# Eight heads per K/V tile and model vectors as rows, in a one-core decode block with adaptive layer norm, cached attention and a gated FFN

## The chip, the core and the metric

The kernel runs on one core of a Trainium2 chip. The core has a matrix engine (PE; its weight loads are shown apart, as PEld), a vector engine (DVE), a scalar engine (ACT), GpSimd (POOL), a queue engine (SP) that issues most transfers, and 16 DMA engines that bring data from device memory (HBM) into the on-chip memory of 128 partitions. Matmul results go to a second memory, PSUM, of eight banks. The metric is the device time of one execution in microseconds; lower is better.

## The reference, cut to what matters

Two tokens (batch `B` = 2, one position each) of width `D` = 640 go through one block. A conditioning vector `c` gives six vectors of width 640 per token. Attention has 32 heads of width 192; each head has its own cache, of which the last `W` = 1024 positions are used. The FFN is 1536 wide.

```python
mod = (silu(c) @ w_mod).reshape(2, 6, 1, -1)
sa, ca, ga, sb, cb, gb = (mod[:, i] for i in range(6))
h = layernorm(x) * (1 + ca) + sa
q = (h @ wq).reshape(2, 1, 32, 192).transpose(0, 2, 1, 3)
k, v = k_cache[:, :, -1024:], v_cache[:, :, -1024:]
p = softmax(einsum('bhqd,bhkd->bhqk', q, k) * 192 ** -0.5)
x = x + ga * (einsum('bhqk,bhkd->bhqd', p, v).transpose(0, 2, 1, 3).reshape(2, 1, 6144) @ wo)
h = layernorm(x) * (1 + cb) + sb
x = x + gb * ((gelu(h @ w_gate) * (h @ w_up)) @ w_down)
```

The caches' part is 50.3 MB, `wq` and `wo` 7.9 MB each, `w_mod` 4.9 MB, the three FFN matrices 2.0 MB each: 76.9 MB in all, each byte read once.

## The kernel before

**Order of work.** The program is a list of operations, each with an engine, the buffers it reads and writes, and a name. Each engine runs its own operations in the order in which they were listed, and waits (L93) for those of other engines that it depends on. So the order of the listing is the order of every queue. SP issues the transfers (L231) and, in its own order, waits for the slot that a transfer will fill.

**Stages.** `w_mod` comes first, then `wq` in five pieces, then K and V, `wo` in six pieces, `w_gate`, `w_up`, and `w_down` in three pieces. Vectors of width 640 are kept as columns: 128 partitions, five values each per token. `mod_part` (L359), the `wo` product (L556) and the `down` product (L606) therefore load a 128x128 piece of the weights into PE and stream two columns (the tokens) through it. `ln_norm` makes the layer norm's sums with one matmul against ones (L311) and a chain of small DVE operations; `ln_mod` applies scale and shift and gives the columns that the next product streams. The q product (L382) is turned round: the two token columns are the loaded operand, `wq` streams, in four column tiles of PE side by side (partitions 0, 32, 64, 96 of the output). `q_unit` spreads q over the partitions, two of the eight units before the loop and the rest within it.

**Ring.** `wq`, K, V and `wo` pass through a ring of `NS` = 8 slots of 12 KB per partition. A slot is refilled by the item eight places later in `items`, once its reader is done (`declare_ring`).

**Attention loop.** One K or V tile holds `HQ` = 4 heads of one token; a partition holds 32 consecutive positions of one head, one run of 12,288 bytes. There are `NG` = 16 groups. For group g, DVE multiplies K by q (`d_mul`, L419) in three pieces of 16, 8 and 8 positions; PE sums each piece over the head width with 12 matmuls against the identity (`p_reduce`, L432); DVE finishes the sum (L439) and takes a maximum (L442); PE transposes it (L444), DVE takes the maximum per head (L449), PE spreads it (L458, L459), DVE subtracts it (L464), ACT takes the exponent and its sum (L467); PE adds the sums over partitions (L473) and multiplies with V (`p_pv`, L484, four column tiles); DVE inverts the sum (L493), ACT scales the result (L495), and PE places it (`p_sel`, L507). The loop at L514 is written out as a pipeline of three groups: while DVE multiplies group g's three pieces, the sum, maximum and subtraction of group g-1 stand between the pieces, and inversion and placing of group g-2 too.

**Tail.** The ACT copy of all heads' result (L546), `wo` (L556), the residual (L574, L577), the second layer norm, gate and up products (`ffn_gu`, L587, 60 load-and-matmul pairs each, weight columns 12 elements apart), GELU (L594), the gating product (L598), the down product (L606), the last residual (L612, L615), and one transfer of the result (L617).

Of the kernel before, what the change touches and what calls it, by code (L numbers as in the profile page):

```python
# [103 lines left out]
def bass_adaLN_cond__sliding_block_cached__geglu_ffn__decode_kernel(  # L104
# [22 lines left out]
    HQ = 4  # L127
# [5 lines left out]
    DD = Dh // NT  # L133
    FC = F // P
    assert B == 2 and D == KT * P and J * PH == W and NQD * HQ == H and NT * P == NQ
    assert DD * NT == Dh and DD * H == P and FC * P == F and J % 8 == 0
# [3 lines left out]
    GC = 512 // J  # L140
    NCH = Dh // GC
    assert GC * NCH == Dh
# [3 lines left out]
    NS = 8  # L146
    SLOT = J * Dh
    assert SLOT == NQ
    WOT = 8
    NWO = NT // WOT  # L150
    assert NWO * WOT == NT and WOT * D <= SLOT
    CHUNKS = [(0, J // 2), (J // 2, J // 4), (3 * J // 4, J // 4)]
    WD_SPLIT = [(0, 6), (6, 4), (10, 2)]
    assert FC == 12
    X0 = HQ * DD * (NQD - 1) + DD - 1
    ZW = X0 + DD * (HQ - 1) + P
    QW = 2 * Dh
    NQB = NQ // (HQ * QW)

    es = ExitStack()  # L160
    with es:
# [10 lines left out]
        prod = sb("prod", [P, 2, J, Dh], BF16)  # L172
        qbc = sb("qbc", [P, B, NQD, Dh], BF16)
        qrow = sb("qrow", [P, NQ // HQ], BF16)
# [4 lines left out]
        mask4 = sb("mask4", [P, HQ], F32)  # L179
        mneg = sb("mneg", [P, HQ], BF16)  # L180
        maskc = sb("maskc", [P, P], F32)
        selq = sb("selq", [P, B, P], BF16)
        ztmp = sb("ztmp", [P, 4, 2, HQ], BF16)
        zsel = sb("zsel", [P, 2, ZW], BF16)
        rows = sb("rows", [2 * B, D], BF16)
        scT = sb("scT", [P, KT, B], BF16)
        X2 = sb("X2", [P, 2, KT, B], F32)
        st4 = sb("st4", [P, 4], F32)
        mv = sb("mv", [P, 8], F32)
        rstd = sb("rstd", [P, 2], F32)  # L190
        modT = sb("modT", [P, 6, KT, B], F32)
        opc = sb("opc", [P, 2, KT, B], F32)
        lnt = sb("lnt", [P, 2, KT, B], F32)
# [13 lines left out]
        fin = sb("fin", [P, KT, B], F32)  # L207
        finb = sb("finb", [P, B, KT], BF16)
        ps = es.enter_context(nc.psum_tensor("ps", [P, 8, 512], F32))

        BK_S = (0, 1)
        BK_Q = (2, 3)
# [3 lines left out]
        BK_M = 7  # L216

# [3 lines left out]
        sem_x = S.sem("d_x")  # L221
# [6 lines left out]
        sem_out = S.sem("d_out")  # L228
# [4 lines left out]
        items = [("wq", k) for k in range(KT)] + [("k", 0)]  # L233
        for g in range(1, NG):
            items += [("k", g), ("v", g - 1)]
        items += [("v", NG - 1)] + [("wo", i) for i in range(NWO)]
# [6 lines left out]
        def ring_src(it):  # L243
            kind, i = it
            if kind == "wq":
                return A_wq.rearrange("(p k) n -> p k n", k=KT)[:, i, :], NQ
            if kind == "wo":
                return A_wo.rearrange("(p t) n -> p t n", t=NT)[:, i * WOT:(i + 1) * WOT, :].rearrange("p t n -> p (t n)"), WOT * D
            quad, b = group(i)
            src = A_k_cache if kind == "k" else A_v_cache  # L250
            return src[b, quad * HQ:(quad + 1) * HQ, K0:Sk, :].rearrange("h (p j) d -> p h (j d)", p=PH), SLOT

        def declare_ring(consumed=()):
            ring_state["done"].update(consumed)
            while ring_state["next"] < len(items):
# [8 lines left out]
        S.dma("act", k_dma(rows[0:B, :], c[:, :]), sem_c, writes=["rows"], name="ld_c")  # L264
        S.dma("act", k_dma(rows[B:2 * B, :], A_x.rearrange("b o d -> (b o) d")), sem_x, writes=["rows_x"], name="ld_x")
        wm_dma = S.dma("sp", k_dma(wm_v.rearrange("p k n -> p (k n)"), w_mod.rearrange("(p k) n -> p (k n)", k=KT)), sem_wm,
                       writes=["wm"], name="ld_wm")
        declare_ring()

# [6 lines left out]
             reads=["ident_f"], writes=["ident_b"], name="ident_b")  # L276
        for b in range(B):
            S.op("pool", lambda e, b=b: e.affine_select(out=selq[:, b, :].rearrange("p (x h) -> p x h", h=HQ),
                                                        in_=ones_b[:, 0:1].unsqueeze(2).broadcast_to([P, PH, HQ]),
                                                        pattern=[[0, PH], [-32, HQ]],  # L280
                                                        compare_op=ALU.is_equal, fill=0.0, base=-b, channel_multiplier=1),
                 reads=["ones_b"], writes=[("selq", b)], name="selq%d" % b)
        S.op("pool", lambda e: e.affine_select(out=ztmp[:, :, :, :].rearrange("p i q h -> p i (q h)"),
                                                in_=ones_b[:, 0:1].unsqueeze(2).broadcast_to([P, 4, 2 * HQ]),
                                                pattern=[[-32, 4], [-1, 2 * HQ]],
# [4 lines left out]
        S.op("dve", lambda e: e.memset(ps[:, 0:4, 0:QW], 0.0), writes=[bank(k) for k in range(4)], name="init_Q")  # L290
        S.op("dve", lambda e: e.memset(ps[:, BK_O, 0:ON], 0.0), writes=[bank(BK_O)], name="init_O")
        S.op("dve", lambda e: e.tensor_reduce(out=mask4[:, :], in_=ident_f[:, :].rearrange("p (x h) -> p h x", h=HQ), axis=AX.X, op=ALU.add),
             reads=["ident_f"], writes=["mask4"], name="mask4")

        cx_ps = ps[:, BK_M, 256:256 + 2 * KT].bitcast(BF16).rearrange("p (j r) -> p j r", j=KT)

        def cx_T(e):
            last = None
            for j in range(KT):
                last = e.transpose(cx_ps[:, j, :], rows[:, :].rearrange("r (p j) -> r p j", j=KT)[:, :, j], ident_b[0:2 * B, 0:2 * B])  # L300
            return last
        S.op("pe", cx_T, reads=["rows", "rows_x", "ident_b"], writes=[bank(BK_M)], name="cxT")
        S.op("act", lambda e: e.activation(out=scT[:, :, :], in_=cx_ps[:, :, 0:B], func=ACTF.Silu),
             reads=[bank(BK_M)], writes=["scT"], name="silu")
        S.op("dve", lambda e: e.tensor_copy(out=X2[:, 0, :, :], in_=cx_ps[:, :, B:2 * B]),
             reads=[bank(BK_M)], writes=[("X2", 0)], name="x_f32")

        def ln_norm(tag):
            S.op("dve", lambda e: e.tensor_tensor(out=X2[:, 1, :, :], in0=X2[:, 0, :, :], in1=X2[:, 0, :, :], op=ALU.mult),
                 reads=[("X2", 0)], writes=[("X2", 1)], name=tag + "_sq")  # L310
            S.op("pe", lambda e: e.matmul(ps[:, BK_M, 448:448 + 4 * KT], lhsT=ones_f[:, :],  # L311
                                          rhs=X2[:, :, :, :].rearrange("p q j b -> p (q j b)"), start=True, stop=True),
                 reads=[("X2", 0), ("X2", 1), "ones_f"], writes=[bank(BK_M)], name=tag + "_stat")
            S.op("dve", lambda e: e.tensor_reduce(out=st4[:, :].rearrange("p (q b) -> p q b", q=2),
                                                  in_=ps[:, BK_M, 448:448 + 4 * KT].rearrange("p (q j b) -> p q b j", q=2, j=KT),
                                                  axis=AX.X, op=ALU.add),
                 reads=[bank(BK_M)], writes=["st4"], name=tag + "_sum")
            S.op("dve", lambda e: e.tensor_scalar(out=mv[:, 0:4], in0=st4[:, :], scalar1=1.0 / D, scalar2=None, op0=ALU.mult),
                 reads=["st4"], writes=[("mv", 0)], name=tag + "_mean")
# [15 lines left out]
        def ln_mod(tag, opc_idx, s_idx, dst_bf):  # L335
# [13 lines left out]
             reads=["ztmp", "zsel"], writes=["zsel"], name="zsel")  # L349

        mod_pe = []

        def mod_part(part, i0, i1):
            def f(e):
                last = None
# [43 lines left out]
        def q_unit():  # L399
            if qstate["n"] >= len(qunits):  # L400
                return
# [268 lines left out]
```

## Time and profile before

| what | value |
|---|---|
| time, median of 3 runs | 195.16 us (195.07 to 195.35) |
| the profiled execution's own time | 194.89 us |
| its span, first to last instruction | 193.1 us |
| bytes read from HBM | 76.88 MB, 398 GB/s over the span |
| busy: PE, DVE, ACT | 124.5, 86.4, 28.3 us |
| mean clock granted to PE | 0.862 of full speed |
| second piece of `wq` done to third, third to fourth, fourth to fifth: starts of the q product | 26.98, 30.67, 34.36 us |
| DVE starts on K of group 0, of group 1 | 38.01, 41.69 us |
| DVE starts on K of group 15 | 146.48 us |
| last piece of `wo` is multiplied | 172.50 to 174.26 us |
| `w_gate` product, `w_up` product | 177.77 to 181.52, 181.80 to 185.56 us |
| result's transfer is issued | 188.90 us |

An instruction group is listed with its line, engine, operation, what it writes and reads, its shape and count, and then its busy time, the mean length of one, and the idle time before it with what ended that. In a chain of waits each step goes back to what released the step after it. The granted clock is written down by the profiler from 44.1 us on; what stands before that as full speed has no record behind it.

### The profile page before, as it was taken

What the parts mean: (1) busy time and instruction counts of PE and PEld (TensorE: products, weight loads), DVE (VectorE), ACT (ScalarE), POOL (GpSimd) and SP (SyncE); (2) the same over time, 40 slices, a digit from 0 to 9 for tenths busy, and PEclk for the clock granted to TensorE, in tenths of its full rate; (3) what the DMA queues carried; (4) which work ended last, traced back from release to release, by engine and by line L of the source; (5) the groups of instructions that cost most, each with busy time, mean ns of one, the idle gap of its engine ahead of it and who ended that gap; (6) DMA issues with size and microseconds to landing.
All of it is one profiled execution on the core that took longest, in us unless ns stands there. A gap on an engine that the chain in (4) does not pass through costs nothing.

```text
span 193.1 us, 3891 instructions
## 1 busy us (share of the span) xinstructions
PE 124.5 (64%) x1723; PEld 95.2 (49%) x1723; DVE 86.4 (45%) x164; ACT 28.3 (15%) x70; POOL 2.6 (1%) x12
## 2 busy tenths in 40 slices
PE   0108932479768777597597586596595858563990
PEld 0108600158446556475375355384374538463990
DVE  3221000396847747658649549559556600004000
ACT  2300000303211312201101101201111231003000
POOL 5000000000000000000000000000000000000000
PEclk9999999999996999969879999969969975555555
DMA  7999999999999999999999999999999999999910
GB/s 255 438 392 428 426 428 425 423 428 428 428 421 428 426 425 419 431 417 433 416 433 420 426 422 422 428 422 428 421 425 428 420 415 431 414 435 423 378 71 1
DMA packets 7353, 77.13 MB, mean 399 GB/s; under 512 B 1060, under 2 KB 1064, under 8 KB 1448
## 3 DMA queue, kind: packets, MB, share of 16 engines
q1 hardware_dynamic: 7328, 76.88, 94.7%
q8 instruction: 13, 0.21, 0.4%
q14 instruction: 4, 0.03, 0.0%
q10 hardware_dynamic: 8, 0.01, 0.0%
HBM read 76.88 MB, written 0.00 MB: 398 GB/s over the span
## 4 chain that ended last, share of the span: by engine, by line
DMA 81%; DVE 6%; PE 6%; issue 3%; SPq 1%; DVEq 0%
DMA ring<-in_A_k_cache_dram 53%; DMA r<-in_B_w_up_dram 15%; DMA ring<-in_A_wq_dram 13%; DVE prod L419 4%; PE ps L587 2%; PE ps L432 1%; PE ps L606 1%; SPq L231 1%; DVE S_sb L439 1%; PE ps L382 1%; DVE nmx L449 0%; DVE M L442 0%; DVE rden L493 0%; DVE aT L598 0%; DVE finb L615 0%
## 5 line engine op out<-in xcount | busy, mean ns | idle before, releaser
L432 PE MATMUL ps<-prod,ident_b 128*128 128x128 bf16 (+1 forms) x576 | 59.1, 261 | 28.1 <-DVE prod L419 28.0
L419 DVE TENSOR_TENSOR prod<-ring,qbc 128x1536 bf16<-128x1536 bf16 (+1 forms) x48 | 58.1, 1214 | 26.4 <-DMA ring<-in_A_k_cache_dram 26.4
L432 PEld LDWEIGHTS ps<-prod,ident_b 128*128 128x128 bf16 x576 | 45.3, 108 | 42.4 <-DVE prod L419 37.8
L495 ACT ACTIVATE On<-ps,rden 128x384 bf16<-128x384 f32 x16 | 9.3, 580 | 42.8 <-DVE rden L493 39.5
L556 PE MATMUL ps<-oT,ring 128*128 128x2 bf16 x240 | 10.4, 179 | 5.3 <-DMA ring<-in_A_wo_dram 4.9
L484 PE MATMUL ps<-ring,E_sb 128*8 128x384 bf16 x256 | 13.4, 330 | 0.0
L556 PEld LDWEIGHTS ps<-oT,ring 128*128 128x128 bf16 x240 | 10.0, 131 | 5.8 <-DMA ring<-in_A_wo_dram 5.2
L467 ACT ACTIVATE E_sb<-Sb_sb 128x128 bf16<-128x128 f32 x16 | 4.9, 309 | 47.1 <-DVE Sb_sb L464 47.1
L382 PE MATMUL ps<-ring,hT 128*2 128x384 bf16 x80 | 7.1, 517 | 7.2 <-DMA ring<-in_A_wq_dram 7.2
L439 DVE TENSOR_REDUCE S_sb<-ps 128x32 f32<-128x512 f32 x16 | 10.8, 673 | 1.3 <-PE ps L432 1.3
L359 PE MATMUL ps<-scT,r 128*128 128x2 bf16 x150 | 6.3, 179 | 6.4 <-DMA r<-in_w_mod_dram 6.2
L359 PEld LDWEIGHTS ps<-scT,r 128*128 128x128 bf16 x150 | 6.2, 131 | 6.6 <-issue 6.3
L587 PE MATMUL ps<-h2T,r 128*128 128x2 bf16 x120 | 7.5, 199 | 2.5 <-DVE h2T L338 2.2
L587 PEld LDWEIGHTS ps<-h2T,r 128*128 128x128 bf16 x120 | 7.3, 164 | 2.7 <-DVE h2T L338 2.3
L574 DVE TENSOR_TENSOR lnt<-ps,modT 128x10 f32<-128x10 f32 x1 | 0.2, 169 | 17.9 <-PE ps L556 17.9
L473 PE MATMUL ps<-denp,maskc 128*128 128x1 f32 x32 | 6.1, 260 | 3.0 <-ACT E_sb L467 2.6
L382 PEld LDWEIGHTS ps<-ring,hT 128*2 128x2 bf16 x80 | 2.1, 108 | 11.5 <-DMA ring<-in_A_wq_dram 9.5
L464 DVE TENSOR_TENSOR Sb_sb<-S_sb,ps 128x128 f32<-128x128 f32 x16 | 4.6, 288 | 6.4 <-PE ps L459 6.4
L473 PEld LDWEIGHTS ps<-denp,maskc 128*128 128x128 f32 x32 | 4.8, 188 | 5.3 <-ACT E_sb L467 5.2
L393 DVE CAST qrow<-ps 128x384 bf16<-128x384 f32 x2 | 1.0, 553 | 13.8 <-PE ps L382 13.8
L458 PE MATMUL ps<-nmx,ones_f 1*128 1x4 f32 x32 | 6.5, 271 | 0.4 <-DVE nmx L449 0.4
L449 DVE TENSOR_REDUCE nmx<-ps 1x4 f32<-1x128 f32 x16 | 4.5, 278 | 4.7 <-PE ps L444 4.7
(64 smaller groups left out, 75.9 us busy)
## 6 DMA issues: line engine op xcount, KB each, us to landing
ring<-in_A_k_cache_dram SPq DMA_DIRECT2D x16, 1536.0 KB, 24.9
ring<-in_A_v_cache_dram SPq DMA_DIRECT2D x16, 1536.0 KB, 26.0
ring<-in_A_wq_dram SPq DMA_DIRECT2D x5, 1536.0 KB, 24.7
ring<-in_A_wo_dram SPq DMA_DIRECT2D x6, 1280.0 KB, 24.0
r<-in_w_mod_dram SPq DMA_DIRECT2D x1, 4800.0 KB, 14.2
r<-in_B_w_gate_dram SPq DMA_DIRECT2D x1, 1920.0 KB, 25.6
r<-in_B_w_up_dram SPq DMA_DIRECT2D x1, 1920.0 KB, 29.7
r<-in_B_w_down_dram SPq DMA_DIRECT2D x1, 960.0 KB, 31.6
```

Source lines behind the costliest of these rows:

```text
L359: last = e.matmul(ps[:, BK_M, (i * KT + j) * 2:(i * KT + j) * 2 + 2], lhsT=wm_v[:, k, i * D:(i + 1) * D].rearrange("p (m j) -> p m j", j=K ...
L382: last = e.matmul(ps[32 * i:32 * i + B, n, 0:QW].rearrange("p (q d) -> p q d", d=Dh), lhsT=hT[:, k, :], rhs=wv[:, 2 * n:2 * n + 2, i, :], ...
L419: S.op("dve", lambda e: e.tensor_tensor(out=prod[:, z, j0:j0 + nj, :], in0=ring[:, sl, j0 * Dh:(j0 + nj) * Dh].rearrange("p (j d) -> p j d ...
L432: last = e.matmul(o_ap, lhsT=ident_b[:, :], rhs=prod[:, z, j0:j0 + nj, t * GC:(t + 1) * GC], start=(ci == 0 and t == 0), stop=(t == NCH - ...
L439: S.op("dve", lambda e: e.tensor_reduce(out=S_sb[:, z, :], in_=ps[:, BK_S[z], :].rearrange("p (j c) -> p j c", c=GC), axis=AX.X, op=ALU.ad ...
L458: e.matmul(o_ap, lhsT=ones_f[0:1, :], rhs=nmx[:, z, :], start=True, stop=False)
L467: S.op("act", lambda e: e.activation(out=E_sb[:, z, :, :], in_=Sb_sb[:, z, :, :], func=ACTF.Exp, scale=SCALE, accum_out=denp[:, z:z + 1]), ...
L473: S.op("pe", lambda e: e.matmul(ps[:, BK_T, P + 8:P + 9], lhsT=maskc[:, :], rhs=denp[:, z:z + 1], start=True, stop=True), reads=[("denp", ...
L484: last = e.matmul(ps[32 * i:32 * i + 2 * HQ, BK_O, 0:ON], lhsT=E_sb[:, z, 2 * jp:2 * jp + 2, :].rearrange("p j h -> p (j h)"), rhs=ring[:, ...
L495: S.op("act", lambda e: e.activation(out=On[:, z, :], in_=ps[:, BK_O, 0:ON], func=ACTF.Identity, scale=rden[:, z:z + 1]), reads=[bank(BK_O ...
L556: last = e.matmul(ps[:, BK_M, 2 * j:2 * j + 2], lhsT=wv[:, tl, :, j], rhs=oT[:, t, :], start=(t == 0 and j == 0), stop=(t == NT - 1), skip ...
L587: last = e.matmul(ps[:, bk, fc * 2:fc * 2 + 2], lhsT=wv[:, k, :].rearrange("p (m f) -> p m f", f=FC)[:, :, fc], rhs=h2T[:, k, :], start=(k ...
```

## The change

Each K or V tile holds eight heads: a partition holds 64 positions of one head, a run of 24,576 bytes, and there are 8 groups in place of 16. The ring has 4 slots of 24 KB. `wq` comes in three pieces, `wo` in three (19, 19 and 10 of its 48 rows per partition). The loop lists one group after the other: two pieces of 32 positions are multiplied and summed, then the whole softmax, the V product and the inversion of that group, and only then the next group's first piece. All of q is spread before the loop.

Vectors of width 640 are kept as rows: 160 values on each of the partitions 0, 1, 32, 33, 64, 65, 96, 97 (token and quarter). The products with `w_mod`, `wo` and `w_down` load the token columns and stream the weights in four column tiles, as the q product does. The layer norm's sum of squares is taken on ACT, and its output goes back to columns by 20 small matmuls. The gate and up weights are taken with columns 3 elements apart; `w_down` is laid out to match, with runs of 3,840 bytes. The result leaves in two transfers of four runs of 320 bytes, from SP and from ACT; `x` comes in by two such transfers.

```diff
-    HQ = 4
+    NR = 4
+    DR = D // NR
+    HQ = 8
-    NS = 8
+    NS = 4
...
-    CHUNKS = [(0, J // 2), (J // 2, J // 4), (3 * J // 4, J // 4)]
-    WD_SPLIT = [(0, 6), (6, 4), (10, 2)]
+    WD_SPLIT = [(0, 2), (2, 1), (3, 1)]
...
-        items = [("wq", k) for k in range(KT)] + [("k", 0)]
-        for g in range(1, NG):
-            items += [("k", g), ("v", g - 1)]
-        items += [("v", NG - 1)] + [("wo", i) for i in range(NWO)]
+        items = [("wq", k) for k in range(NWQ)]
+        for g in range(NG):
+            items += [("k", g), ("v", g)]
+        items += [("wo", i) for i in range(NWO)]
...
+        def ln_stats(tag):
+            S.op("act", lambda e: e.activation(out=sqj[:, :], in_=X[:, :], func=ACTF.Square, accum_out=st2[:, 1:2]),
...
+            S.op("dve", lambda e: e.tensor_reduce(out=st2[:, 0:1], in_=X[:, :], axis=AX.X, op=ALU.add),
...
+            S.op("pe", lambda e: e.matmul(ps[:, BK_M, CS:CS + 2], lhsT=selstat[:, :], rhs=st2[:, :], start=True, stop=True, skip_group_check=True),
...
+            S.op("dve", lambda e: e.tensor_copy(out=mv[:, :], in_=ps[:, BK_M, CS:CS + 2]),
...
+        def ln_mod(tag, opc_idx, s_idx, dst_bf):
...
+                hv = hrow[:, :].rearrange("p (m j) -> p m j", j=KT)
+                for j in range(KT):
+                    for i in range(NR):
+                        last = e.matmul(ps[32 * i:32 * i + 32, BK_M, CT + 2 * j:CT + 2 * j + 2], lhsT=hv[:, :, j], rhs=selrow[:, i, :],
...
+        for half in range(2):
+            def f(e, half=half):
...
+                        last = e.matmul(ps[32 * i:32 * i + B, half, 0:MH].rearrange("p (m n) -> p m n", n=DR), lhsT=scT[:, k, :],
+                                        rhs=wv[:, 3 * half:3 * half + 3, i, :],
...
+        S.op("dve", lambda e: e.memset(ps[:, 5:8, :], 0.0), writes=[bank(k) for k in range(5, 8)], name="init_O2")
...
+            S.op("dve", lambda e: e.tensor_tensor(out=prod[:, ci, :, :],
+                                                  in0=ring[:, sl, ci * JC * Dh:(ci + 1) * JC * Dh].rearrange("p (j d) -> p j d", d=Dh),
+                                                  in1=qbc[:, b, quad, :].unsqueeze(1).broadcast_to([P, JC, Dh]), op=ALU.mult),
...
+        for g in range(NG):
+            for ci in range(NCK):
+                d_mul(g, ci)
+                p_reduce(g, ci)
+            declare_ring([("k", g)])
+            if g:
+                p_sel(g - 1)
+            c_soft(g)
+            p_pv(g)
+            declare_ring([("v", g)])
+            c_on(g)
+        p_sel(NG - 1)
...
+                    for i in range(NR):
+                        last = e.matmul(ps[32 * i:32 * i + B, BK_M, 0:DR], lhsT=oT[:, t, :], rhs=wv[:, tl, i, :],
+                                        start=(t == 0), stop=(t == NT - 1), tile_position=(0, 32 * i))
...
-                                        lhsT=wv[:, k, :].rearrange("p (m f) -> p m f", f=FC)[:, :, fc],
+                                        lhsT=wv[:, k, a * P * FR:(a + 1) * P * FR].rearrange("p (m r) -> p m r", r=FR)[:, :, r],
...
+                    for i in range(NR):
+                        last = e.matmul(ps[32 * i:32 * i + B, BK_OT, CY:CY + DR], lhsT=aT[:, fc, :], rhs=wv[:, i, :],
...
+        for b in range(B):
+            S.dma(("sp", "act")[b], k_dma(out[b, 0, :].rearrange("(i n) -> i n", i=NR), finb[b:P:32, :]), sem_out[b], reads=["finb"], name="st_out%d" % b)
```

`c_soft(g)` lists, for one group and in this order, what L439, L442, L444, L449, L458, L459, L464, L467 and L473 did, on 64 positions and 8 heads; `c_on(g)` what L493 and L495 did.

## The prediction, made before the changed kernel ran

> **What bounds the kernel now.** I read the chain of waits first, then the waits themselves.
>
> ```profile
> DMA 81%; DVE 6%; PE 6%; issue 3%; SPq 1%; DVEq 0%
> ```
>
> ```profile
> PE ps L432 <- DVE prod L419: 28.0, 25, 2.3
> DVE prod L419 <- DMA ring<-in_A_k_cache_dram: 26.4, 16, 2.5
> ```
>
> The DMA stream sets the end (81%). In the loop DVE waits for each of the 16 K tiles, 1.65 us on average, so compute keeps up with room to spare: the starts on K of groups 1 and 15 (41.69 and 146.48 us) are 14 groups apart, 7.48 us a group, or 14.97 us per eight heads. The pipelined listing is what earns this room. So I ask what one eight-head group costs once its steps stand in line.
>
> The groups by shape give the lengths:
>
> ```profile
> L432 PE MATMUL ps<-prod,ident_b 128*128 128x128 bf16 x384 | 30.1, 236 | 1.9 <-DVE prod L419 1.7
> L419 DVE TENSOR_TENSOR prod<-ring,qbc 128x1536 bf16<-128x1536 bf16 x32 | 30.1, 942 | 0.0
> L432 PE MATMUL ps<-prod,ident_b 128*128 128x256 bf16 x192 | 29.3, 313 | 26.3 <-DVE prod L419 26.3
> L419 DVE TENSOR_TENSOR prod<-ring,qbc 128x3072 bf16<-128x3072 bf16 x16 | 28.1, 1758 | 26.4 <-DMA ring<-in_A_k_cache_dram 26.4
> L439 DVE TENSOR_REDUCE S_sb<-ps 128x32 f32<-128x512 f32 x16 | 10.8, 673 | 1.3 <-PE ps L432 1.3
> ```
>
> and the timeline of the last group, where nothing else is in the way, gives the softmax with its hand-overs (start, length, engine, line):
>
> ```profile
> 154.02 0.28 DVE L449 TENSOR_REDUCE nmx<-ps 1x4 f32<-1x128 f32 x1 [0.36 <-PE ps L444]
> 154.36 0.38 PE L458 MATMUL ps<-nmx,ones_f 1*128 1x4 f32 x2 [0.37 <-DVE nmx L449]
> ...
> 154.95 0.29 DVE L464 TENSOR_TENSOR Sb_sb<-S_sb,ps 128x128 f32<-128x128 f32 x1 [0.65 <-PE ps L459]
> 155.27 0.31 ACT L467 ACTIVATE E_sb<-Sb_sb 128x128 bf16<-128x128 f32 x1 [1.01 <-DVE Sb_sb L464]
> ...
> 155.73 0.38 PE L473 MATMUL ps<-denp,maskc 128*128 128x1 f32 x2 [0.88 <-ACT E_sb L467]
> ...
> 156.22 0.17 DVE L493 RECIPROCAL rden<-ps 128x1 f32<-128x1 f32 x1 [0.98 <-PE ps L473]
> ```
>
> The reader is to see that the inversion comes 2.2 us after the per-head maximum. In the changed listing it stands on DVE ahead of the next group's first multiplication: the next K tile, landed or not, queues behind it.
>
> **The loop, part by part (period C per eight heads).** At full clock:
> - Multiplications: 1,536 to 3,072 elements cost 0.82 us more, so 6,144 take 3.39. The second starts 3.31 after the first (each starts some 0.08 before the end of the one ahead) and ends at 6.70.
> - The second piece's reduction starts 0.05 later. Twelve matmuls of 512 columns: at full clock they start 109 ns apart at 256 columns and some 56 at 128, so 216 at 512; 2.59, with the last one's drain 2.75.
> - Sum over 1,024 PSUM values: 0.67 + 0.53 (512 more at 1.04 ns, as 673 ns for 512 has it); maximum 0.22; hand-overs: transpose 1.56 after the reduction's end, and 0.30 to the per-head maximum.
> - Per-head maximum to subtraction 0.93 as shown; subtraction on 512 in place of 128 values 0.32 + 0.40; exponent to sum matmul 0.46 + 0.32 (384 more at 0.83, from ACT's 0.31 for 128 and 0.58 for 384, the dearer row, as the upper end 0.40); inversion 0.49 later, and 0.09 to the next multiplication.
>
> Together 6.70 + 0.05 + 2.75 + 1.56 + 0.30 + 0.93 + 0.72 + 0.78 + 0.58 = 14.4 us.
>
> **The clock** comes on top. Of the reductions (L432) alone, and with the granted clock behind the counts:
>
> ```profile
> 54.40:57.80 3.40, 0.20 (x4) 0.02 (x1) 1.00 1.02 424
> 57.90:61.10 3.20, 2.56 (x12) 1.67 (x13) 0.50 1.00 422
> 92.00:95.40 3.40, 0.03 (x1) 0.03 (x2) 0.99 1.02 430
> 95.50:98.70 3.20, 3.19 (x18) 2.24 (x18) 0.50 1.02 424
> 119.30:122.60 3.30, 1.63 (x24) 1.30 (x24) 1.00 1.02 432
> 122.70:126.10 3.40, 1.22 (x11) 1.09 (x12) 0.99 1.02 424
> 126.20:129.40 3.20, 2.63 (x23) 2.05 (x22) 0.50 1.00 422
> ```
>
> A stretch of 3.4 us with 1.2 us of reductions or less (second column) was followed by 3.4 us at half clock, one with 1.63 was not; after a stretch full of them full clock came back. The old loop goes without reductions for 3.7 us at the most that I found (91.7 to 95.4). The new one does, from the end of the second reduction to the next first one: softmax 4.9 and a multiplication 3.4, 8.3 us, which holds a whole such stretch every time. So I take each first reduction to begin at half clock (427 ns a matmul: at 58.5 us twelve of 256 took 2.74 us). In the old trace full clock came 2.7 to 4.4 us after the reductions began. With 2.7: 6.3 slow and 5.7 fast matmuls, 3.93 in place of 2.59, of which the second multiplication hides 0.77: +0.6. With 4.4: 4.77, +1.4. Middle +1.0, and 0.1 for slower small matmuls: **C = 15.5**. Ends: 14.4 with no slow stretch; 16.6 if the return is a further 1 us late and half of that falls on the second reduction.
>
> [...]
>
> **DMA.** Eight runs per engine of 12,288 bytes take 3.69 us (q product's starts), of 10,240 take 3.09 (`wo`'s waits), so a run costs 11 ns plus 36.6 per thousand bytes, and one of 24,576 about 911 ns against 922 for two halves. K and V save 128 x 11 ns = 1.4 us, `wq` and `wo` 0.45: 1.85 us by the last `wo` piece, a K/V pace of 14.75 us per eight heads. Ends: 0 (runs gain nothing) and 2.5. As C > 14.75, the loop falls behind from the first group, 0.75 us each, 5 by the last. The ring does not run dry for that: K of group g+2 is issued 6.7 us into group g, with V of g+1 still to land, 22 us after K of g; lags under 10 us cost the stream nothing. So the saving is hidden: compute, not landing, sets the end.
>
> **Head.** First K tile (old groups 0 and 1): 41.69 - 0.3 = 41.35. All q units now stand before it: q product done at 35.6, four pairs of q matmuls at 0.33 each with their copies to 39.6, the PSUM clearing (1.34, as L290) to 41.0. It fits by 0.3 us; if not, each us of it is a us at the end. The `w_mod` product, 40 matmuls of 480 columns in four tiles, 4.0 at half clock for 6.3 before, and 1.7 us more of layer norm are covered by the wait for `wq`.
>
> **Tail, from the last V product's end:**
> - 1.7 to the first `wo` matmul, as before (157.27 to 159.00).
> - `wo`: 192 load-and-matmul pairs. Not in the trace in this form: by L556 40 ns a pair (40 in 1.76 us), by the q product streaming 384 columns 80 ns, so 160 columns 33. I take 40: 7.9. Ends 6.4 and 12 (60 ns, as L587).
> - Second layer norm, 3.5 before: DVE steps on 160 values 0.33 in place of 0.17 (five: +0.8), square and its sum on ACT 0.5 for 0.2, output matmuls 20 x 40 ns + 0.2 and a copy 0.25, less one step and the two scalings 0.7: 4.9.
> - Gate and up: 60 ns a pair at 12 columns apart, 40 at five apart (L556, L606); I take 40 for three apart: 2 x 2.6 = 5.2 for 7.5.
> - Gating 0.3; down 48 pairs 2.1 for 2.6; last residual 0.75 for 0.4.
> - Result: 4.2 from 188.9 to the span's end, unchanged; bounds 3.0 and 5.0, since 256 short runs become 8 on two queues.
>
> 27.1 in all. The V product ends 2.1 us after the last period (32 column-tile matmuls, 1.6 at full clock, 2.8 at half). The span ends at 41.35 + 8C + 2.1 + 27.1; the profiled time is 1.8 above its span (194.89 against 193.1) and the median 0.3 above that. So **time = 72.6 + 8C**: 196.6 for C = 15.5, equal to before at 15.3.
>
> **Rivals.**
> 1. The clock mostly holds or returns early, C at or under 15.1, and the stream paces: last `wo` piece at 172.50 - 1.85 = 170.65, its 40 pairs 1.8, then 4.9 + 5.2 + 0.3 + 2.1 + 0.75 + 4.2 to 189.9: **192.0**, up to 194.2 at C = 15.2. For: stretches at 47.5 and 105.6 held under 1 us of reductions and kept full clock. Against: the 8.3 us gap. 34%.
> 2. Half clock reaches into every second reduction, C over 16: at 16.3, **203.0**. For: full clock may come back only after a full stretch, 4.4 us as at 81 us. Against: 2.7 was seen too. 14%.
> 3. Long runs bring no DMA rate: 0.3 us on the forecast through the first K tile, 1.9 on rival 1; within the others' chances.
>
> **How the numbers follow.** The forecast, C from 15.2 to 16.0, 194.2 to 200.6, has 52%; its own time 196.6. The measurement tells 0.2% (0.4 us) from no change: faster is rival 1 and the forecast's lowest part, 38%; within, C from 15.27 to 15.37, 6%; slower 56%. The range 192.0 to 202.0 leaves out the lowest of rival 1 and most of rival 2 beyond.
>
> **What would show it.** DVE's waits for K tiles gone after the first groups, and its starts on K 15 to 16 us apart; first reductions at half clock, second mostly at full; `wo` pieces landed before they are asked for; the chain naming DVE and PE in place of DMA. I am wrong if DVE still waits for K at the last group, if a pair of `wo` costs 60 ns or more, or if the first K tile waits for q.

## The result and the profile after

The changed kernel took **306.23 us** (303.89 to 309.61, four runs), the kernel before, run beside it, 195.12 (194.81 to 195.35): a ratio of 1.566, with a 95% interval of 1.556 to 1.575. The ratio leaves out the longest of the four, 309.61 us, which ran in a slower state. The forecast was 196.6. The profiled execution has a span of 302.2 us.

The chain of waits of the changed kernel, its shares by engine:

```profile
DMA 54%; another core or an unknown queue 17%; PE 13%; DVE 13%; ACT 1%; SPq 1%; issue 1%; DVEq 0%
```

DMA still leads, and the forecast was that it would not. (The 17% without a name are stretches such as 95.47 to 108.46 us in which this view names no releaser; the DVE timeline below names the K tile as the end of that one.) The two rows of the page that say what DMA did, in 40 slices of 7.6 us (busy share of the 16 engines in tenths, then what they moved):

```profile
DMA  8999999999999999999999999999999999999992
GB/s 321 422 423 417 291 218 215 208 218 220 215 218 218 211 224 218 218 220 211 224 218 221 221 218 224 218 221 224 228 218 228 227 221 215 207 419 415 426 406 89
```

and the GB/s of the kernel before, in slices of 4.8 us:

```profile
GB/s 255 438 392 428 426 428 425 423 428 428 428 421 428 426 425 419 431 417 433 416 433 420 426 422 422 428 422 428 421 425 428 420 415 431 414 435 423 378 71 1
```

Read together these are the result. The engines are busy in every slice. In slices 2 to 4 (`w_mod`, `wq`) and 36 to 39 (`wo`, FFN) they move some 420 GB/s; between lie K and V, at some 218. The kernel before held 416 to 433 through K and V. So the engines do not lack work. The same work takes them twice as long, in K and V alone. In the packet records of the trace a run of 24,576 B of `wq` takes 912 ns; one of K or V, of the same size, 1,866 (medians).

DVE's multiplications, from the timeline (start, length; idle time before in brackets):

```profile
50.37 6.63 DVE L449 TENSOR_TENSOR prod<-ring,qbc 128x6144 bf16<-128x6144 bf16 x2 [7.35 <-DMA ring<-in_A_k_cache_dram]
79.39 6.63 DVE L449 TENSOR_TENSOR prod<-ring,qbc 128x6144 bf16<-128x6144 bf16 x2 [13.77 <-DMA ring<-in_A_k_cache_dram]
108.46 3.36 DVE L449 TENSOR_TENSOR prod<-ring,qbc 128x6144 bf16<-128x6144 bf16 x1 [12.99 <-DMA ring<-in_A_k_cache_dram]
```

The first K tile is there 9.0 us later than forecast (50.37 for 41.35), a group then takes 28.6 us (50.37 to 250.81 for seven) in place of 15.5, and DVE waits for K every time. These two account for 9.02 + 7 x 13.13 = 100.9 of the 107.7 us between the forecast span (41.35 + 8 x 15.5 + 2.1 + 27.1 = 194.5) and the measured one; the rest, some 6.7 us, lies after the last K tile, where the `wo` product now waits for its pieces (8.7 us in all).

### The profile page after: what moved, and what is told of

The parts are those of the page before. It is cut to its first block, busy times and chain, and to the rows that moved or that the text cites. A ratio compares the mean times of both kernels' runs of the same rounds, so it can differ in the third digit from the quotient of the medians.

```text
span 302.2 us, 2476 instructions
## 1 busy us (share of the span) xinstructions
PE 121.7 (40%) x1097; PEld 56.9 (19%) x1097; DVE 86.2 (29%) x91; ACT 22.7 (8%) x46; POOL 3.8 (1%) x17
## 4 chain that ended last, share of the span: by engine, by line
DMA 54%; another core or an unknown queue 17%; PE 13%; DVE 13%; ACT 1%; SPq 1%; issue 1%; DVEq 0%
DMA ring<-in_A_k_cache_dram 32%; DMA r<-in_B_w_down_dram 13%; PE ps L461 10%; DMA ring<-in_A_wq_dram 10%; DVE prod L449 9%; DVE S_sb L468 2%; ACT E_sb L487 1%; SPq L246 1%; DVE Sb_sb L484 1%; PE ps L417 1%; PE ps L490 1%; PE ps L481 1%; DVE nmx L475 0%; PE ps L473 0%
## 5 line engine op out<-in xcount | busy, mean ns | idle before, releaser
L461 PE MATMUL ps<-prod,ident_b 128*128 128x512 bf16 x192 | 59.1, 481 | 108.5 <-DVE prod L449 108.5
L449 DVE TENSOR_TENSOR prod<-ring,qbc 128x6144 bf16<-128x6144 bf16 x16 | 53.0, 3355 | 95.8 <-DMA ring<-in_A_k_cache_dram 95.8
L461 PEld LDWEIGHTS ps<-prod,ident_b 128*128 128x128 bf16 x192 | 22.1, 119 | 147.1 <-DVE prod L449 114.1
L501 PE MATMUL ps<-ring,E_sb 128*16 128x384 bf16 x256 | 21.9, 522 | 0.1
L468 DVE TENSOR_REDUCE S_sb<-ps 128x64 f32<-128x1024 f32 x8 | 9.8, 1225 | 33.7 <-PE ps L461 33.7
L487 ACT ACTIVATE E_sb<-Sb_sb 128x512 bf16<-128x512 f32 x8 | 5.0, 629 | 189.3 <-DVE Sb_sb L484 189.3
L555 PE MATMUL ps<-ring,oT 128*2 128x160 bf16 x192 | 6.9, 336 | 8.7 <-DMA ring<-in_A_wo_dram 8.7
L501 PEld LDWEIGHTS ps<-ring,E_sb 128*16 128x16 bf16 x256 | 7.9, 124 | 8.7 <-issue 8.4
L555 PEld LDWEIGHTS ps<-ring,oT 128*2 128x2 bf16 x192 | 5.9, 121 | 9.5 <-DMA ring<-in_A_wo_dram 9.5
L484 DVE TENSOR_TENSOR Sb_sb<-S_sb,ps 128x512 f32<-128x512 f32 x8 | 5.5, 687 | 5.5 <-PE ps L482 5.5
L473 PE MATMUL ps<-ident_f,M 128*1 128x128 f32 x8 | 2.2, 270 | 11.2 <-DVE M L471 11.2
L511 DVE RECIPROCAL rden<-ps 128x1 f32<-128x1 f32 x8 | 1.4, 169 | 11.8 <-PE ps L490 11.8
```

Source lines behind the costliest of these rows:

```text
L449: S.op("dve", lambda e: e.tensor_tensor(out=prod[:, ci, :, :], in0=ring[:, sl, ci * JC * Dh:(ci + 1) * JC * Dh].rearrange("p (j d) -> p j ...
L461: last = e.matmul(o_ap, lhsT=ident_b[:, :], rhs=prod[:, ci, :, t * GC:(t + 1) * GC], start=(t == 0), stop=(t == NCH - 1))
L468: S.op("dve", lambda e: e.tensor_reduce(out=S_sb[:, z, :], in_=ps[:, 2 * z:2 * z + 2, :].rearrange("p k (j c) -> p (k j) c", c=GC), axis=A ...
L484: S.op("dve", lambda e: e.tensor_tensor(out=Sb_sb[:, z, :, :], in0=S_sb[:, z, :].unsqueeze(2).broadcast_to([P, J, HQ]), in1=ps[:, BK_T, P: ...
L487: S.op("act", lambda e: e.activation(out=E_sb[:, z, :, :], in_=Sb_sb[:, z, :, :], func=ACTF.Exp, scale=SCALE, accum_out=denp[:, z:z + 1]), ...
L501: last = e.matmul(ps[32 * i:32 * i + 2 * HQ, BK_O, 0:ON], lhsT=E_sb[:, z, 2 * jp:2 * jp + 2, :].rearrange("p j h -> p (j h)"), rhs=ring[:, ...
```

## The experiments

Eight heads in a tile change three things in a K/V transfer: the run doubles, eight far-apart heads take turns where it was four, and the source pattern has 16 rows (16 positions' blocks, each of 8 heads) in place of 32 rows of 4. Three theories, one for each: LONG RUNS, FAR HEADS, SIXTEEN ROWS. All DMA rates below are means from 60 to 160 us, where K and V are on the way (in the runs at the full rate `wo` too, from 149 us). Runs 1 to 12 are one execution each, beside the kernel before on the same chip; the rates that they are read for differ by nearly a factor of two or more. In the runs with "near" data K and V are read from neighbouring places of the caches, so their numbers are others than the reference's; the rest of the work is the same. The kernel before took 193.96 to 194.26 us on these chips.

**1. Half-length runs.** Each tile by two transfers, [16 rows][8 heads][12,288 B]. An entry names first and last partition, first and last column, and source.

```diff
-            return src[b, quad * HQ:(quad + 1) * HQ, K0:Sk, :].rearrange("h (p j) d -> p h (j d)", p=PH), SLOT
+            v = src[b, quad * HQ:(quad + 1) * HQ, K0:Sk, :].rearrange("h (p j) d -> p h (j d)", p=PH)
+            return [(0, P, c * SLOT // 2, (c + 1) * SLOT // 2, v[:, :, c * SLOT // 2:(c + 1) * SLOT // 2]) for c in range(2)]
```

> Each K/V tile comes in two transfers of 12,288-byte runs (16 rows of 8 heads each) in place of one with 24,576-byte runs; partitions and heads as in the changed kernel. Three theories of why the K/V stream runs at 218 GB/s in place of 425. LONG RUNS (the run of 24,576 bytes at a pitch of 24,576 is slow by itself): about 425 GB/s in the loop, about 198 us. FAR HEADS (engines that work side by side read heads that are whole multiples of 1.57 MB apart and get in each other's way in HBM): unchanged, 218 GB/s, about 306 us. SIXTEEN ROWS (the source pattern's outermost count is 16, not 32, so the tile is dealt to the 16 engines in blocks of eight neighbouring partitions, and engines that work side by side meet at the same part of the on-chip memory): unchanged, 218 GB/s, about 306 us.

299.51 us. The stretch of K and V (start and end, length, busy time and count of PE, PEld, DVE, ACT, POOL, granted clock, DMA share, GB/s; this column order holds for all such lines):

```profile
60.00:160.00 100.00, 40.87 (x254) 17.59 (x252) 30.18 (x26) 5.21 (x12) 0.00 (x0) 0.65 1.01 221
```

The old run length, and still 221 GB/s: LONG RUNS is out.

**2. Four heads at a time.** Heads 0 to 3 into partitions 0 to 63, heads 4 to 7 into 64 to 127, [16 rows][4 heads][24,576 B] each; the masks stay, so the result is not the reference's.

```diff
+            return [(64 * s, 64 * s + 64, 0, SLOT, src[b, quad * HQ + 4 * s:quad * HQ + 4 * s + 4, K0:Sk, :].rearrange("h (p j) d -> p h (j d)", p=PH))
+                    for s in range(2)]
```

> Each K/V tile comes in two transfers, heads 0 to 3 to partitions 0 to 63 and heads 4 to 7 to partitions 64 to 127 (16 rows of 4 heads each, runs of 24,576 bytes); the masks of the softmax are left as they are, so heads are mixed up in what is computed and the amount of work is the same. FAR HEADS, if what hurts is that two engines read heads four apart: 425 GB/s, about 198 us. LONG RUNS: 218 GB/s, about 306 us. SIXTEEN ROWS: each engine has four neighbouring partitions now, but all 16 write into one half of the partitions at a time; between 218 and 425 GB/s, nearer to 218, so 250 to 306 us.

304.21 us:

```profile
60.00:160.00 100.00, 41.07 (x254) 17.88 (x252) 30.19 (x26) 5.21 (x12) 0.00 (x0) 0.66 1.00 216
```

Four heads in turn did not help either; but this run also fills only half of the partitions at a time, so it settles little by itself.

**3 and 4. Near data, as 16 rows of 8 and as 128 plain rows.** The runs of a tile lie 24,832 B apart, so nothing is far; only the way in which the pattern is written differs.

```diff
+            v = flat[o:o + PH * EP].rearrange("(p m) -> p m", p=PH)[:, 0:HQ * RP]
+            return v.rearrange("p (h n) -> p h n", h=HQ)[:, :, 0:SLOT], SLOT
...
+            return flat[o:o + P * RP].rearrange("(p n) -> p n", n=RP)[:, 0:SLOT], SLOT
```

> Each K/V tile is read from 128 runs of 24,576 bytes that lie close together (24,832 bytes apart, so other data than the reference's) through a pattern of 16 rows of 8, as the changed kernel's pattern has it. No two engines read heads that are far apart. FAR HEADS: 425 GB/s, about 198 us. SIXTEEN ROWS: 218 GB/s, about 306 us. LONG RUNS: 425 GB/s if the pitch of exactly 24,576 is needed for it, 218 if the length alone does it.

> The control of the run before: the same runs of 24,576 bytes, 24,832 bytes apart, through a pattern of 128 rows (other data than the reference's). All theories but LONG RUNS by length alone: 425 to 430 GB/s, and then the time of the changed kernel without its slow stream, which shows what a period of the loop costs: by the prediction's sum with C = 15.5 and the tail as the changed kernel's profile has it (some 3 us shorter than predicted) about 193 to 197 us.

310.83 and 195.31 us. The stretch of the first, then of the second:

```profile
60.00:160.00 100.00, 41.34 (x259) 18.09 (x257) 30.19 (x26) 5.21 (x12) 0.00 (x0) 0.66 1.00 210
```

```profile
60.00:160.00 100.00, 71.78 (x441) 31.24 (x434) 59.24 (x44) 8.40 (x19) 0.00 (x0) 0.76 1.00 429
```

FAR HEADS is out: near data in 16 rows of 8 are as slow (210 GB/s). Written as 128 rows they come at 429 GB/s, a run in 915 ns. Run 4 also has the changed kernel's four slots, so those do not starve the stream. It is also the changed kernel as the prediction imagined it, with the stream at full pace; it is used for the rest of the working below.

**5. Near data as 32 rows of 4** (long runs, the old count of rows).

```diff
+            v = flat[o:o + 32 * EP].rearrange("(p m) -> p m", p=32)[:, 0:4 * RP]
+            return v.rearrange("p (h n) -> p h n", h=4)[:, :, 0:SLOT], SLOT
```

> The changed kernel with K/V runs of 24,576 B that lie near one another (24,832 B from run to run), as in the run with 128 rows, but written as 32 rows of 4 runs: the count of rows that the kernel before has, with the run length of the change. The K/V numbers are other data than the reference's. SIXTEEN ROWS (only a first count of 16 is slow): about 430 GB/s through K/V, a run in about 911 ns, the time that of the 128-row run, 195.3 us (194 to 197). If instead every pattern of more than one level pays in proportion to how few rows it has (16 rows a factor of two, 32 rows something between): 250 to 380 GB/s and 210 to 270 us.

194.99 us:

```profile
60.00:160.00 100.00, 71.75 (x443) 31.31 (x436) 59.10 (x44) 8.39 (x19) 0.00 (x0) 0.76 1.00 429
```

Two levels do no harm by themselves (429 GB/s, as with 128 rows).

**6. Near data, two transfers of 64 plain rows,** into partitions 0 to 63 and 64 to 127.

```diff
+            return [(64 * s, 64 * s + 64, 0, SLOT, v[64 * s:64 * s + 64, 0:SLOT]) for s in range(2)]
```

> The changed kernel with each K/V tile loaded by two transfers of 64 plain rows (24,576 B each, near one another), one into partitions 0 to 63, one into 64 to 127. Again other data than the reference's. SIXTEEN ROWS: 64 is not 16, so about 430 GB/s and 195 to 198 us (sixteen more issues on SP, which waits anyway). Rival HALF: a transfer into half of the partitions is what is slow, which the run with two transfers of 16 rows of 4 could not tell apart from its 16 rows: about 218 GB/s and 300 to 310 us.

311.2 us:

```profile
60.00:160.00 100.00, 40.51 (x255) 17.77 (x252) 30.20 (x26) 5.21 (x12) 0.00 (x0) 0.64 1.00 211
```

SIXTEEN ROWS fails: 64 plain rows are as slow (211 GB/s), if they fill one half of the partitions. And HALF alone cannot be it, since 16 rows of 8 fill all 128.

**7. The kernel before, with each tile cut into two transfers of 16 rows of 4.** Nothing else changes.

```diff
+            v = src[b, quad * HQ:(quad + 1) * HQ, K0:Sk, :].rearrange("h (p j) d -> p h (j d)", p=PH)
+            return [(64 * s, 64 * s + 64, SLOT, v[16 * s:16 * s + 16]) for s in range(2)]
```

> The kernel before, nothing of the change in it, but each K/V tile of four heads loaded by two transfers of 16 rows of 4 runs of 12,288 B, into partitions 0 to 63 and 64 to 127; every byte goes from where to where it went before. SIXTEEN ROWS: the K/V stream falls to about 218 GB/s (14.4 us per four heads where it had 7.4), DVE waits for K, and the time is 290 to 305 us. Rival (the slow stream needs something of the changed kernel, such as its four-slot ring or its runs of 24,576 B): the time stays at 194 to 197 us.

288.63 us, just under the range expected, with 240 GB/s through K and V. Its waits (in total, times, longest):

```profile
DVE prod L420 <- DMA ring<-in_A_k_cache_dram: 97.5, 15, 8.1
```

In the kernel before this wait was 26.4 us. The slow stream needs nothing of the changed kernel: every byte goes where it went before, and only which partitions are filled by one transfer differs. That alone costs a tuned kernel 94 us. Why it ran at 240 and not at 218 is open.

**8. The changed kernel with four heads in a tile again** (32 rows of 4); rows, stride 3, store and unpipelined loop are kept.

```diff
-    HQ = 8
+    HQ = 4
...
-    JC = 32
+    JC = 16
...
-    NS = 4
+    NS = 8
```

> The changed kernel with four heads in a tile again (32 rows of 4 runs of 12,288 B, eight slots) and all the rest of the change: rows, stride 3, row store, and its loop without overlap of two tiles. SIXTEEN ROWS: K/V come at about 425 GB/s. Then the loop is set by compute: per four heads 3.4 (multiply) + 1.7 (reduction behind the second multiply, at full clock) + 0.6 + 0.35 (sum, subtract: half of the eight-head ones) + about 2.3 (the small steps, which do not shrink with the tile) = 8.4 us at full clock, up to 9.0 with half clock at the reductions; 16 of these in place of 8 of 15.67 in the 128-row run add 9 to 19 us: 204 to 214 us. Rival (the four slots, not the rows, starve the stream): then eight slots help here too and the two theories agree, but DVE would still wait for K now and then.

235.08 us: the stream is cured (some 425 GB/s up to 93 us, where the loop falls so far behind that the ring is full), the compute estimate missed. The groups by line:

```profile
L460 PE MATMUL ps<-prod,ident_b 128*128 128x512 bf16 x192 | 70.6, 544 | 19.2 <-DVE prod L448 19.2
L467 DVE TENSOR_REDUCE S_sb<-ps 128x32 f32<-128x1024 f32 x16 | 19.6, 1225 | 45.5 <-PE ps L460 45.5
```

With `JC` 16 the two pieces' sums still fill two whole banks, so neither the sum (1,225 ns, I had 0.6 us) nor the matmuls' width was halved, and a reduction's matmul took longer in the mean (544 ns against 460 in run 5; clock granted from 60 to 160 us 0.74 against 0.76). A group of four heads took 9.3 to 11.8 us, 10.4 on average, in place of 8.4 to 9.0. So the tile of eight does what it was meant to do for an unpipelined loop; the loop of three groups in flight does at least as much (run 13).

**9. Where the writes go.** Each run so far fits one rule: what counts is which partitions are written at the same moment. The rate was half with 64 neighbouring partitions at a time (211 GB/s, run 6) and full with 128 plain rows (429, run 4). The theory WAYS reads this as ways into the on-chip memory that neighbouring partitions share. The ways are an assumption of mine: no run shows them, and no run before this one gives a rate for 16 neighbours. Near data, eight transfers of 16 plain rows, into 16 neighbouring partitions each:

```diff
+            return [(16 * s, 16 * s + 16, 0, SLOT, v[16 * s:16 * s + 16, 0:SLOT]) for s in (0, 2, 1, 3, 4, 6, 5, 7)]
```

> The changed kernel with each K/V tile loaded by eight transfers of 16 plain rows of 24,576 B, each into 16 neighbouring partitions (near data, other numbers than the reference's). After rows64_two the first count of the pattern no longer explains everything: 64 plain rows into half of the partitions were as slow as 16 rows of 8 into all. New theory WAYS: the rate goes with how many of the on-chip memory's ways in are written at the same moment; groups of partitions share a way, the partitions 0 to 63 reach only half of the ways, and 16 rows of 8 also use only half at any moment because each row of 8 neighbours is worked off by one engine in step with the others. [...] Rival COUNT (a count of 16 halves, wherever it goes): 218 GB/s and 300 to 312 us. Rival SHARE (rate in proportion to the share of the partitions written, 16 of 128): 54 GB/s and about 1000 us.

502.03 us:

```profile
60.00:160.00 100.00, 24.04 (x132) 10.13 (x132) 18.41 (x14) 2.61 (x6) 0.00 (x0) 0.59 1.01 118
```

118 GB/s is 0.275 of 429 and 0.56 of the 211 that 64 neighbours got; it is neither the 218 of COUNT nor the 54 of SHARE. That fewer neighbours get a lower rate fits WAYS.

**10. Both halves on two queues.** Run 2 with the second transfer of each tile issued by ACT.

```diff
-                    S.dma("sp", k_dma(ring[p0:p1, slot, c0:c1], src), sem_ring[slot][c], writes=[("ring", slot, c)], name="ld_%s%d" % items[n])
+                    S.dma(("sp", "act")[c], k_dma(ring[p0:p1, slot, c0:c1], src), sem_ring[slot][c], writes=[("ring", slot, c)], name="ld_%s%d" % items[n])
```

> The kernel two64 (16 rows of 4 runs of 24,576 B into partitions 0 to 63, and as many into 64 to 127; masks as in the change, so the numbers are others) with the second transfer of each tile issued on ACT's queue in place of SP's: same patterns, same counts, same partitions, same bytes, but both halves of the partitions can now be written at the same time. WAYS: the stream goes well above 218 GB/s, up to 430, and the time falls from 304 to 196 to 235 us. Rival COUNT: still 16 rows, still about 218 GB/s and 300 to 310 us.

285.85 us and 234 GB/s: neither theory's number. The packets under way by queue, counted in the trace's packet records at eight moments:

```
at us         104.5  105.5  106.0  107.0  107.5  108.5  109.5  110.5
SP's queue       14      6      0     10     16     12      2      8
ACT's queue       2     10     16      6      0      4     14      8
```

The engines swing between the two queues, but seldom all together: between 60 and 160 us both queues had packets under way in 96% of the moments, so both halves were being written. Still a run took 1,681 ns (median), little less than the 1,891 of run 2 and far from 915. Why is not shown, and the run does not tell the theories apart.

**11 and 12. The same 16 rows, and 32, spread out.** Near data; eight transfers of 16 rows into every eighth partition, and four of 32 rows into every fourth (the entries now hold the partition step as well).

```diff
+            return [(s, P, 8, 0, SLOT, v[s:P:8, 0:SLOT]) for s in range(8)]
...
+            return [(s, P, 4, 0, SLOT, v[s:P:4, 0:SLOT]) for s in range(4)]
```

> As rows16_eight (eight transfers of 16 plain rows of 24,576 B per K/V tile), but each transfer goes into every eighth partition (s, s+8, ..., s+120) in place of 16 neighbours. This is the order in which 16 rows of 8 are written if each of 16 engines works off one row from its first run to its last. [...] WAYS: about 218 GB/s, the pace of the changed kernel itself, and 300 to 315 us. Rivals COUNT or SHARE with the neighbours' 117 GB/s (same count, same share of the partitions): 490 to 510 us again.

> [...] WAYS, if the rows are dealt to the engines as in the 32 rows of 4 that ran at full rate: about 430 GB/s and 195 to 198 us, though a transfer reaches half as many partitions as rows64_two's (218 GB/s). [...] Rival SHARE (32 of 128 partitions): 108 GB/s and about 530 us.

310.72 and 195.01 us. The stretch of the first, then of the second:

```profile
60.00:160.00 100.00, 42.37 (x263) 18.56 (x261) 30.20 (x26) 5.18 (x12) 0.00 (x0) 0.65 1.00 212
```

```profile
60.00:160.00 100.00, 71.28 (x438) 31.23 (x435) 59.61 (x44) 8.41 (x19) 0.00 (x0) 0.76 1.00 426
```

Run 9 and run 11 differ in nothing but which 16 partitions, and with them which 16 source rows, belong together: 118 against 212. A transfer of run 12 fills 32 partitions and has the full rate, one of run 6 fills 64 and has half. So it is neither the count of rows nor the number of partitions, but the set written at once. Runs 11 and 12 came out as WAYS has them (about 218, and about 430 if the 32 rows are dealt to the engines as in run 5), and not as its rivals do (117 for run 11 by COUNT or SHARE, 108 for run 12 by SHARE).

A rival is that the source rows read together decide, and not the partitions. No run moved the partitions and left the source rows together as they were. But the source alone was changed: the 16 rows of 8 ran at 218 GB/s from far heads and 210 from near data (run 3), half of the partitions at 216 from far heads (run 2) and 211 from near rows (run 6), and 32 rows of 4 at some 425 from far heads (the kernel before, in shorter runs) and 429 from near data (run 5). The rate went with the partitions each time.

For the change itself this reads as follows. Run 11 writes in the order in which 16 rows of 8 would be written if each of 16 engines worked off one row, all in step: 0, 8, 16, ... together, then 1, 9, 17, ... It has the change's pace, 212 to 218. That the engines are in fact given one row each is inferred; the packet records do not name the engine. Nor is it shown in which order 128 plain rows are written, which have the full rate (429, run 4). No run tried a mended layout of the eight-head tile on the reference's own data.

**13. Rows of the change, tile and loop of before,** and **14. the kernel before with stride 3 in the FFN alone.**

```diff
-    HQ = 8
+    HQ = 4
...
-    NS = 4
+    NS = 8
...
-        for g in range(NG):
-            items += [("k", g), ("v", g)]
+        items += [("k", 0)]
+        for g in range(1, NG):
+            items += [("k", g), ("v", g - 1)]
```

Run 13, against the changed kernel (and the loop of the kernel before, as listed there). Run 14, against the kernel before:

```diff
-                                        lhsT=wv[:, k, :].rearrange("p (m f) -> p m f", f=FC)[:, :, fc],
+                                        lhsT=wv[:, k, a * P * FR:(a + 1) * P * FR].rearrange("p (m r) -> p m r", r=FR)[:, :, r],
...
-        wd_src = B_w_down.rearrange("(p f) n -> p f n", f=FC)
+        wd_src = B_w_down.rearrange("(a p r) n -> p a (r n)", a=FA, r=FR)
```

> A version that might beat both: the kernel before's K/V tile, slots and loop (four heads, 32 rows of 4, two tiles overlapped), with the change's row vectors, stride 3 and row store. Before, the last piece of w_down landed at about 186 us and the span ended at 193.1; the bytes are the same, so it lands at about 186 here too. Behind it, from the change's profiles: the last piece's matmuls 0.4, the two residual steps 0.7, the store from issue to end 2.35: 189.5 us of span, 191.5 us, 1.4% under the kernel before (189.5 to 193). Rival: the longer second layer norm of the rows (5.35 in place of 3.4) and the pause of PE in the wo part (3.4 us in rows128) put the end on compute again: no gain, 193.5 to 196.

> The kernel before with nothing of the change but the FFN columns at stride 3 and the w_down order that goes with it. Gate and up fall from 3.75 to about 1.8 us each; up then waits for w_up (landed at about 181.3) and down for the last piece of w_down (186.0), of which only the last 15 pairs (0.65) stay behind the landing: the residual starts at about 186.8 in place of 188.5, with the old store 4.2: span 191.4, 193.3 us, 0.9% under the kernel before (192.4 to 194). If the hybrid gains and this doesn't, the gain is the row store's and the rows'.

Run 13: 192.19 us, 0.990 of the kernel before (0.989 to 0.992). Run 14: 192.86, 0.993 (0.992 to 0.995). Both take less time than both kernels. The end of run 13, then of run 14, from the timeline:

```profile
182.04 1.76 PE L619 MATMUL ps<-h2T,r 128*128 128x2 bf16 x60 [1.12 <-DMA r<-in_B_w_up_dram]
...
186.73 0.57 PE L639 MATMUL ps<-r,aT 128*2 128x160 bf16 x12 [0.60 <-DMA r<-in_B_w_down_dram]
...
188.06 0.66 SPq L247 DMA_DIRECT2D out_dram<-finb  x1
```

```profile
181.98 1.76 PE L588 MATMUL ps<-h2T,r 128*128 128x2 bf16 x60 [2.21 <-DMA r<-in_B_w_up_dram]
...
186.62 0.76 PE L607 MATMUL ps<-aT,r 128*128 128x2 bf16 x15 [0.28 <-DMA r<-in_B_w_down_dram]
...
187.84 0.40 SPq L232 DMA_DIRECT2D out_dram<-finb  x1
```

In both the `w_up` product and the last piece of `down` wait for their weights: the tail is now bound by the stream's last byte, at about 186.6 us. Run 14 even issues its result earlier. Run 13 is ahead by the store: 2.4 us from its issue to the end of the span (190.5), against 3.3 in run 14 (191.1) and 4.2 in the kernel before. The expectations were 0.7 too low for run 13 (the last weights came 0.7 later than in the kernel before) and 0.4 too high for run 14 (a store 0.9 cheaper than assumed, weights 0.6 later).

## Why the prediction was wrong, step by step

**The step that failed** is the DMA part: "so a run costs 11 ns plus 36.6 per thousand bytes, and one of 24,576 about 911 ns against 922 for two halves", and the "K/V pace of 14.75 us per eight heads" taken from it. The price of a run is right where the stream has its full rate (912 for `wq`, 915 in run 4). It was fitted on `wq` and `wo`, transfers with 128 plain rows, and carried to 16 rows of 8 without asking where these rows land. There a run took 1,866 ns and eight heads' K and V 28.6 us. Rival 3 only asked whether the runs would gain nothing; no case had the stream become slower.

With that, "compute, not landing, sets the end" and "the ring does not run dry" fell for the changed kernel, as did the first K tile: not q held it up, as the last sentence feared, but its landing. The first of the prediction's own signs of being wrong came: DVE waited 11.94 us for the K of the last group.

**What run 4 shows of the other steps,** with the stream at full pace. The DVE timeline:

```profile
41.60 6.62 DVE L452 TENSOR_TENSOR prod<-ring,qbc 128x6144 bf16<-128x6144 bf16 x2 [1.82 <-DMA ring<-in_A_k_cache_dram]
58.02 6.61 DVE L452 TENSOR_TENSOR prod<-ring,qbc 128x6144 bf16<-128x6144 bf16 x2
72.40 6.61 DVE L452 TENSOR_TENSOR prod<-ring,qbc 128x6144 bf16<-128x6144 bf16 x2
88.95 6.61 DVE L452 TENSOR_TENSOR prod<-ring,qbc 128x6144 bf16<-128x6144 bf16 x2
```

- *First K tile* 41.60 (41.35 said), and after it no wait for K: compute sets the pace, as said.
- *C*: 16.4, 14.4, 16.6 here, 15.67 as the mean of all seven (15.5 said). The parts measured 3.35 for a multiplication (3.39), 1.23 for the sum (1.2), 0.69 for the subtraction (0.72), 0.63 for the exponent (0.63). The four periods with the half clock at the reductions cost 16.4 to 16.8, the three without 14.4 to 14.5: the two ends of the working. (Granted were 1.00 from 64 to 68 us, in the second period, of 14.4, and 0.50 from 76 to 80, in the third, of 16.6.) So the clock term was about right in mean and wrong in form, some 2.1 us in about every second period in place of 1.0 in each; that the mean came out is luck.
- *The chain* names PE 38%, DVE 31%, DMA 20%, as said.

Its tail, with `wo` first:

```profile
171.72 2.59 PE L558 MATMUL ps<-ring,oT 128*2 128x160 bf16 x140 [0.46 <-ACT oT L548]
177.76 1.90 PE L558 MATMUL ps<-ring,oT 128*2 128x160 bf16 x52 [3.44 <-issue]
```

- *`wo`* took 7.94 us (7.9 said), by two errors that cancel, which is luck: a pair cost 18.5 ns in the first 140 and 37 in the last 52 (36 in the changed kernel, at a granted clock of 0.50), not 40, but PE stood for 3.44 us in the middle, for nothing that the profile names (3.25 in run 5, 1.66 in run 12). The packet records have a 16 KB transfer of an instruction queue at 175.2 us, within that pause; whether PE waits for its code there was not tried.
- *Second layer norm* 5.4 (4.9 said). In the changed kernel the table load that ACT makes between square and root stands in the middle of it:

```profile
288.43 1.28 ACT L355 ACT_TABLE_LOAD   x1 [1.12 <-PE ps L346]
...
289.72 0.20 ACT L355 ACTIVATE st<-nvar 128x1 f32<-128x1 f32 x1
```

- *Gate and up* 3.36 together (5.2 said, 7.5 before): 28 ns a pair at three columns apart, not 40; 1.76 each, 29 ns a pair, in the changed kernel.
- *Down* 1.8 (2.1 said), *last residual* 0.7 (0.75).
- *Result* 2.3 (4.2 said, bounds 3.0 and 5.0): eight runs of 320 bytes on two queues were done 2.3 us after their issue, 256 of 10 on one 4.2 in the kernel before. Here a bound was wrong.

Together: 195.31 us against the 196.6 of the sum, on a chip where the kernel before took 193.96. So with the stream intact the change would have been slower by 0.4 to 0.7% (runs 5, 12 and 4), for the reason given (a loop in line at C of 15.7). The sum of the compute part held within 0.7%, in part by luck: up to the last V product's end run 4 was 2.7 us later than said, and from there on 3.6 shorter. It decided nothing, since the term that was taken as safe, the stream, was off by a factor of two.

## What to carry to other kernels

A transfer's cost was here not only its bytes and the length of its runs (24,576 B in 912 ns for `wq`, in 1,866 for K and V). When a tile's shape changes, work out which partitions are written side by side: 16 rows of 8 neighbours halved the rate (some 218 GB/s in place of 425) while all engines showed as busy (a DMA share of 1.00). Look at GB/s next to the DMA share, slice by slice; a full share at half the GB/s in one stretch, beside a stretch at full rate, was here the sign that the destination pattern of that stretch was at fault.

And take a change apart before it is given up: the rows, the stride and the store were worth 1.0% once the tile and the pipelined loop were left as they had been.

## What the hardware showed that was not expected

- The rate by the set of partitions written together: 426 to 429 GB/s (128 rows; 32 rows of 4; 32 rows into every fourth), 210 to 221 (16 rows of 8; 64 neighbours; 16 rows into every eighth; 240 in run 7), 118 (16 neighbours).
- The two halves of the partitions loaded one after the other on one queue ran at 216 GB/s; loaded on two queues, both with packets under way, at 234.
- A weight load with columns three apart and its two-column matmul: 29 ns (1.76 us for 60, changed kernel); 63 at twelve apart (3.75 us for 60, kernel before), both at a granted clock of 0.50.
